# Exp of the scores as the stationary operand of the value products, row sums from a column of ones, and results turned afterwards

## The chip, the cores and the metric

One core of one Trainium2 chip. The metric is device time in microseconds (us) of one execution. A kernel is compared with runs of the kernel before on the same chip.

## The reference, cut to what matters

```python
q, k, v: (8, 12, 448, 64)                    # batch, heads, positions, head size
scores = q @ k^T / 8                         # per batch and head
attn   = exp(scores - max); attn /= attn.sum(-1)
x      = (attn @ v) as (8*448, 12*64)        # 3584 tokens, 768 wide
g, val = x @ w_gate, x @ w_val               # 768 -> 1536 each
out    = (silu(g) * val) @ w_out             # 1536 -> 768
```

Attention is followed by a gated FFN. The kernel works in fp16 with fp32 sums in PSUM (the memory that the matmuls write to), and leaves the maximum out of the softmax.

## The kernel before: the parts that matter

The kernel takes heads two at a time: 48 head pairs, six to a batch. The scores are made transposed, in chunks of 112 keys by 2 x 448 queries, four chunks to a pair; ScalarE takes Exp from PSUM to SBUF. `E` is then the *moving* operand: a group of 16 matmuls in four column tiles makes the products of half the head size of two pairs, and another such group, with a stationary operand of ones, their sums. VectorE inverts the sums and multiplies. What comes out is `X`, features on partitions and tokens beside one another, as the FFN wants it.

```python
ps_s = tile_pool(name="ps_s", bufs=3, space=PSUM)     # score tiles AND gate tiles
ps_f = tile_pool(name="ps_f", bufs=2, space=PSUM)     # products, values, outputs
...
def qk(pr, c):                                        # one score chunk
    s = ps_s.tile([128, 2, 512], FP32, tag="s")
    for hx in range(2):
        nc.tensor.matmul(s[:, hx, 0:S], lhsT=<112 keys>, rhs=<448 queries>, ...)
    nc.scalar.activation(E[pr][:, c], s[0:P, :, 0:S], AF.Exp, scale=sm_scale)

def pv(p0, t):                                        # one group of products
    acc = ps_f.tile([128, 512], FP32, tag="f", name="acc")
    for c in range(NC):
        for j in range(4):
            nc.tensor.matmul(acc[ts(j, 32), 0:S], lhsT=<32 value columns>,
                             rhs=E[p0 + j // 2][:, c, j % 2, :], ...)
...
def ffn1_steps(kk, c0, n, hts):
    for fb in range(NFB):
        gp = ps_s.tile([128, 2, 512], FP32, tag="s", name="gp")[:, 0]   # gate
        for cb in range(NCB): mm(gp[:, 0:n], wslice("g", fb, cb), X[...])
        sg = tanh(gp / 2)                                               # ScalarE
        yield
        vp = ps_f.tile([128, 512], FP32, tag="f")                       # value
        for cb in range(NCB): mm(vp[:, 0:n], wslice("v", fb, cb), X[...])
        ...
```

After a first stage of six pairs, in which attention stands alone, the kernel goes in *visits*: score chunks, then sums or products, then FFN matmuls. A visit issues two or (from pair 8 on) three score chunks, then the sums or products that have become due, then a share of FFN matmuls. TensorE executes in that order.

```python
for x, (chunks, todo) in enumerate(plan):
    for pr, c in chunks:
        qk(pr, c)                     # 3 score tiles: the whole ring ps_s
    ...
    while todo:
        product(*todo.pop(0)[1:])     # sums or products, tiles from ps_f
    ...
    run_fv() / run_o()                # FFN: the first thing is a gate tile, from ps_s
```

The softmax here doesn't subtract the row's maximum and nothing guards it: scores larger than these inputs give would overflow.

## Time and profile before

| | before |
|---|---|
| time, median of 3 runs | 459.06 us (458.02 to 460.3) |
| span of the profiled run | 456.6 us |
| attention groups of 16 tiled matmuls | 72 |
| first gate matmul starts | 29.05 us |
| last of the first 24 Exp ends | 26.70 us |
| waits of gate matmuls for Exp | none in the list of waits |

The lines that show where this kernel is bound are in the prediction. One line more, from the timeline of ScalarE, which sets the pace of the first stage (columns: start, length, instruction, count; in brackets the idle time before it and what ended it):

```profile
6.21 16.83 ACT L212 ACTIVATE E<-s 112x896 f16<-112x896 f32 x20
23.36 3.34 ACT L212 ACTIVATE E<-s 112x896 f16<-112x896 f32 x4 [0.32 <-PE s L205]
```

Twenty Exp without a gap, then 0.32 us idle, then four more, which end at 23.36 + 3.34 = 26.70.

### The profile page before, as it was taken

What the parts mean: (1) busy time and instruction counts of PE and PEld (TensorE: products, weight loads), DVE (VectorE), ACT (ScalarE), POOL (GpSimd) and SP (SyncE); (2) the same over time, 40 slices, a digit from 0 to 9 for tenths busy, and PEclk for the clock granted to TensorE, in tenths of its full rate; (3) what the DMA queues carried; (4) which work ended last, traced back from release to release, by engine and by line L of the source; (5) the groups of instructions that cost most, each with busy time, mean ns of one, the idle gap of its engine ahead of it and who ended that gap; (6) DMA issues with size and microseconds to landing.
All of it is one profiled execution on the core that took longest, in us unless ns stands there. A gap on an engine that the chain in (4) does not pass through costs nothing.

```text
span 456.6 us, 17081 instructions
## 1 busy us (share of the span) xinstructions
PE 448.1 (98%) x7808; PEld 249.5 (55%) x7808; DVE 238.8 (52%) x371; ACT 240.4 (53%) x353; POOL 137.7 (30%) x222
## 2 busy tenths in 40 slices
PE   8899999999999999999999999999999999999996
PEld 3355555444466665555556666455555666544564
DVE  2765764666764645655554546645466356354200
ACT  6986657666653655546354555544565542222222
POOL 8555607853470062601625016510300000000000
PEclk9999999999999999999999999999999999999999
DMA  9999999995955269930947359834222010100133
GB/s 133 195 200 201 178 182 178 217 160 80 128 73 78 48 107 121 143 76 9 128 88 97 59 84 135 127 50 76 33 57 57 23 52 20 54 0 1 36 103 105
DMA packets 82984, 44.43 MB, mean 97 GB/s; under 512 B 37600, under 2 KB 79456, under 8 KB 82912
## 3 DMA queue, kind: packets, MB, share of 16 engines
q0 software_dynamic: 43296, 23.37, 40.2%
q1 hardware_dynamic: 39520, 19.92, 23.9%
q8 instruction: 61, 1.00, 0.9%
q14 instruction: 11, 0.09, 0.1%
q10 hardware_dynamic: 96, 0.05, 0.0%
HBM read 47.19 MB, written 11.01 MB: 127 GB/s over the span
## 4 chain that ended last, share of the span: by engine, by line
PE 85%; DMA 12%; POOL 2%; issue 1%; ACT 0%; POOLq 0%
PE gp L280 18%; PE vp L280 18%; PE op L280 18%; PE acc L225 7%; PE s L205 7%; PE op L277 6%; DMA wv<-in_moe_w_val_dram 5%; DMA wo<-in_moe_w_out_dram 4%; PE gp L277 4%; PE vp L277 4%; PE acc L250 4%; DMA wg<-in_moe_w_gate_dram 2%; POOL q L123 1%; POOL k L123 1%; POOL vt L133 0%
## 5 line engine op out<-in xcount | busy, mean ns | idle before, releaser
L212 ACT ACTIVATE E<-s 112x896 f16<-112x896 f32 x192 | 161.7, 921 | 19.2 <-PE s L205 18.9
L280 PE MATMUL gp<-X,wg 128*32 128x384 f16 (+1 forms) x1848 | 100.7, 351 | 0.0
L280 PE MATMUL vp<-X,wv 128*32 128x384 f16 (+1 forms) x1848 | 100.5, 351 | 0.0
L308 DVE SCALAR_TENSOR_TENSOR t<-sg,gp 128x384 f32<-128x384 f32 (+1 forms) x96 | 59.0, 615 | 74.9 <-ACT sg L296 74.9
L296 ACT ACTIVATE sg<-gp 128x384 f32<-128x384 f32 (+1 forms) x96 | 52.7, 549 | 74.2 <-PE gp L280 48.8
L341 ACT ACTIVATE osb<-op 128x384 f32<-128x384 f32 (+1 forms) x57 | 27.7, 485 | 115.8 <-PE op L280 92.0
L280 PE MATMUL op<-wo,hts 128*32 128x384 f16 x1968 | 87.6, 326 | 0.7 <-issue 0.5
L133 POOL DMA_DIRECT2D vt<-in_v_dram x40 | 26.7, 668 | 158.4 <-PE acc L225 149.7
L265 DVE RECIPROCAL R<-ssb 128x112 f32<-128x112 f32 x92 | 72.8, 826 | 0.6
L280 PEld LDWEIGHTS <-wg 128*32 128x32 f16 x1848 | 52.9, 96 | 35.8 <-issue 0.5
L280 PEld LDWEIGHTS <-wv 128*32 128x32 f16 x1848 | 52.9, 97 | 33.5
L280 PEld LDWEIGHTS <-hts 128*32 128x32 f16 x1968 | 57.0, 97 | 25.7 <-issue 1.1
L311 DVE SCALAR_TENSOR_TENSOR hts<-t,vp 128x384 f16<-128x384 f32 (+1 forms) x96 | 59.6, 621 | 10.4 <-DVE t L308 0.5
L239 DVE TENSOR_TENSOR X<-acc,R 128x448 f16<-128x448 f32 x48 | 29.7, 624 | 45.7 <-PE acc L225 42.1
L205 PE MATMUL s<-qkT 64*128 64x448 f16 x384 | 50.4, 353 | 2.6 <-ACT E L212 1.5
L225 PE MATMUL acc<-E,vt 112*32 112x448 f16 x768 | 45.1, 355 | 0.0
L262 DVE COPY ssb<-acc 128x448 f32<-128x448 f32 x23 | 14.4, 625 | 46.9 <-PE acc L250 46.9
L205 PEld LDWEIGHTS <-qkT 64*128 64x128 f16 x384 | 14.8, 94 | 33.2 <-issue 26.7
L123 POOL DMA_DIRECT2D k<-in_k_dram x42 | 27.9, 663 | 12.6 <-DMA wo<-in_moe_w_out_dram 8.9
L277 PE MATMUL op<-wo,hts 128*128 128x384 f16 (+1 forms) x192 | 29.6, 316 | 0.0
L123 POOL DMA_DIRECT2D q<-in_q_dram x42 | 28.1, 668 | 4.2 <-PE s L205 1.4
L225 PEld LDWEIGHTS <-vt 112*32 112x32 f16 x768 | 17.2, 96 | 21.9 <-issue 12.4
(38 smaller groups left out, 217.4 us busy)
## 6 DMA issues: line engine op xcount, KB each, us to landing
q<-in_q_dram POOLq DMA_DIRECT2D x37, 112.0 KB, 4.7
k<-in_k_dram POOLq DMA_DIRECT2D x37, 112.0 KB, 4.9
vt<-in_v_dram POOLq DMA_DIRECT2D x36, 112.0 KB, 4.2
out_dram<-osb SPq DMA_DIRECT2D x7, 336.0 KB, 3.1
wg<-in_moe_w_gate_dram POOLq DMA_DIRECT2D x8, 288.0 KB, 11.0
wv<-in_moe_w_val_dram POOLq DMA_DIRECT2D x8, 288.0 KB, 11.3
wo<-in_moe_w_out_dram POOLq DMA_DIRECT2D x2, 1152.0 KB, 22.9
out_dram<-osb SPq DMA_DIRECT2D x8, 288.0 KB, 3.8
```

What stands on the lines that cost most here:

```text
L123: nc.gpsimd.dma_start(dst[:, ds(h0, 2 * n)], flat.rearrange("h (p c) d -> p h (c d)", c=NC))
L205: nc.tensor.matmul(s[:, hx, 0:S], lhsT=t[ts(hx, 64)].rearrange("p c q -> p (c q)")[:, c * P : c * P + 128], rhs=t[ts(hx, 64), NC:, :].rear ...
L212: nc.scalar.activation(E[pr][:, c], s[0:P, :, 0:S], AF.Exp, scale=sm_scale)
L225: nc.tensor.matmul(acc[ts(j, 32), 0:S], lhsT=v16[g][:, 2 * r + j % 2, c, :].rearrange("p (d t) -> p t d", t=2)[:, t], rhs=E[p0 + j // 2][: ...
L239: nc.vector.tensor_tensor(X[kk][:, hp + t, ts(bb, S)], acc[:, 0:S], R[p0][:], ALU.mult)
L265: lambda i=i: nc.vector.reciprocal(rt[:, ts(i, P)], ssb[:, ts(i, P)]) for i in range(4)
L277: nc.tensor.matmul(dst, lhsT=lhsT, rhs=rhs, start=start, stop=stop)
L280: nc.tensor.matmul(dst[ts(j, 32), :], lhsT=lhsT[:, ts(j, 32)], rhs=rhs, start=start, stop=stop)
L296: nc.scalar.activation(sg[:, 0:n], gp[:, 0:n], AF.Tanh, scale=0.5)
L308: nc.vector.scalar_tensor_tensor(t1[:, 0:n], sg[:, 0:n], 1.0, gp[:, 0:n], ALU.add, ALU.mult)
L311: nc.vector.scalar_tensor_tensor(hts[:, fb, 0:n], t1[:, 0:n], 0.5 * HS, vp[:, 0:n], ALU.mult, ALU.mult)
L341: nc.scalar.activation(osb[:, ds(m0, w)], op[:, 0:w], AF.Copy, scale=1.0 / HS)
```

## The change

Its intent is to make TensorE's attention work cheaper. `E` becomes the *stationary* operand, 128 query columns at a time, and the values the moving one: 64 columns and a 65th of ones, so that each query's row sum comes out beside its result. That takes the 24 groups of sums away. Per pair there are 32 matmuls of 65 columns. The results come out with queries on partitions, so one reciprocal of 7 columns and a scaling finish them there; then they must be turned: TensorE does it for pairs 0 to 11, a DMA transpose after that. So that each stationary operand has a whole 128 columns, `E` has 15 blocks of 64 queries to a key chunk, seven of each head with a block of zeros between; head 0's queries are taken in rotated order, so that the odd blocks of both heads meet in one product, which needs a second copy of the first 64 queries. The FFN is no longer cut into column tiles, and the reciprocal by Ln and Exp on ScalarE with its table load goes.

```diff
-    def pv(p0, t):
+    def pv(pr):
+        e = Es[pr % NE]
+        vo = Vts[pr % NV]                       # values and a column of ones
         acc = ps_f.tile([128, 512], FP32, tag="f", name="acc")
+        a7 = acc[:, 0 : 7 * (D + 1)].rearrange("p (s d) -> p s d", s=7)
         for c in range(NC):
-            for j in range(4):
-                nc.tensor.matmul(acc[ts(j, 32), 0:S], lhsT=v16[...][:, t], rhs=E[...][:, c, j % 2, :], ...)
+            for j in range(3):
+                for hx in range(2):
+                    nc.tensor.matmul(a7[:, 2 * j + hx], lhsT=<2 blocks of e>, rhs=vo[:, hx, c, 0 : D + 1], ...)
+            for hx in range(2):                 # the odd block, with the zeros
+                nc.tensor.matmul(a7[:, 6], lhsT=<2 blocks of e>, rhs=vo[:, hx, c, 0 : D + 1], ...)
+        nc.vector.reciprocal(r[:, 0:7], a7[:, :, D])
+        nc.vector.tensor_tensor(xt[:, 0:3]..., a7[:, 0:6, 0:D], r[:, 0:6]..., ALU.mult)
+        for hx in range(2):
+            nc.vector.tensor_scalar(xt[0:D, 3, ts(hx, D)], a7[ts(hx, D), 6, 0:D], r[...], None, ALU.mult)
+
+    def turn_x(pr):
+        if pr < XPE:                            # XPE = 12
+            ... 4 matmuls with the identity into ps_f, one VectorE copy into X
+            return
+        nc.sync.dma_start_transpose(...)        # two of them
... (cut: sums(), recips(), scaled(), mm() go; buffers, loads of values, copies into Vts)
         for pr in range(FIRST):                 # first stage
-            if pr in (2, 4): sums of two pairs ... products of two pairs
+            if pr in (2, 4): three copy_v
+            pr 2: pv(0); pr 3: pv(1) turn_x(0), turn_x(1) pv(2)
+            pr 4: turn_x(2) pv(3); pr 5: turn_x(3), pv(4)
...
+            if x == 0:
+                turn_x(4); pv(5); turn_x(5)
-            while todo:
-                product(*todo.pop(0)[1:])
+            for _, p0 in todo:
+                pv(p0) ...
```

What the diff does not show at a glance: 72 groups in the visits and the first stage become 48, one to a pair.

More of the change, by code (lines that the diff above doesn't have):

```diff
@@ L23 @@
 FIRST = 6
-TILED = 8
 WIDE = 8
+XPE = 12
+NE = 4
+NX = 3
+NV = 3
+VS = 6
+EB = 15
 @with_exitstack
@@ L65, in load_table @@
         )
-    load_table("natural_log_exp_and_others")
+    load_table("exp_and_others")
     consts = ctx.enter_context(tc.tile_pool(name="consts", bufs=1))
@@ L71 @@
     attp = ctx.enter_context(tc.tile_pool(name="attp", bufs=4))
-    ep = ctx.enter_context(tc.tile_pool(name="ep", bufs=5))
     xp = ctx.enter_context(tc.tile_pool(name="xp", bufs=2))
@@ L77 @@
     ps_f = ctx.enter_context(tc.tile_pool(name="ps_f", bufs=2, space=PSUM))
-    ones = consts.tile([P, 32], FP16, name="ones")
+    Es = [consts.tile([P, NC * EB + 1, D], FP16, name=f"E{i}") for i in range(NE)]
+    Xts = [consts.tile([128, 4, 128], FP16, name=f"xt{i}") for i in range(NX)]
+    Vts = [consts.tile([P, 2, NC, D + 2], FP16, name=f"vo{i}") for i in range(NV)]
+    vraw = consts.tile([P, VS, 2, NC, D], FP16, name="vraw")
     warm = consts.tile([128, 512], FP16, name="warm")
-    ident = consts.tile([P, P], FP16, name="ident")
+    ident = consts.tile([128, 128], FP16, name="ident")
     wgv = {}
@@ L93 @@
     raw = {}
-    v16 = {}
     qkT = {}
-    E = {}
-    R = {}
     X = {}
@@ L126, in load_qk16, with load_v, copy_v @@
             raw[pr + i] = (q16[:, h : h + 2], k16[:, h : h + 2])
-    def load_v(g, lo=0, hi=2 * GP):
-        b = g // GPB
-        h0 = (g % GPB) * 2 * GP
-        if lo == 0:
-            v16[g] = raws.tile([P, 2 * GP, NC, D], FP16, tag="vt", bufs=3, name="vt")
+    def load_v(pr, n=1):
+        b, h = divmod(2 * pr, H)
         nc.gpsimd.dma_start(
-            v16[g][:, lo:hi],
-            v[b, h0 + lo : h0 + hi].rearrange("h (p c) d -> p h (c d)", c=NC),
-        )
+            vraw[:, ds(pr % VS, n)].rearrange("p r h c d -> p (r h) (c d)"),
+            v[b, h : h + 2 * n].rearrange("h (p c) d -> p h (c d)", c=NC),
+        )
+    def copy_v(pr):
+        nc.vector.tensor_copy(Vts[pr % NV][:, :, :, 0:D], vraw[:, pr % VS])
     def load_w(kind, i):
@@ L143, in load_w @@
             src = (moe_w_gate if kind == "g" else moe_w_val)[:, ts(i, DF // 4)].rearrange(
-                "(a p t) m -> t p a m", p=128, t=2
+                "(t a p) m -> t p a m", p=128, t=2
             )
             for t in range(2):
-                nc.gpsimd.dma_start(wgv[kind, i][:, t::2, :], src[t])
+                nc.gpsimd.dma_start(wgv[kind, i][:, ts(t, NCB // 2), :], src[t])
             return
@@ L161, in prep @@
                     nc.gpsimd.tensor_copy(dst, src)
-        qkT[pr] = attp.tile([128, 2 * NC, P], FP16, tag="qkT", name="qkT", bufs=5)
+        qkT[pr] = attp.tile([128, 2 * S + D], FP16, tag="qkT", name="qkT", bufs=5)
         if pr >= NPE:
             nc.sync.dma_start_transpose(
-                qkT[pr][:], qk16[:].rearrange("p t c h d -> p (t c h d)")
+                qkT[pr][:, 0 : 2 * S].rearrange("p (c q) -> p c q", q=P),
+                qk16[:].rearrange("p t c h d -> p (t c h d)"),
+            )
+            nc.sync.dma_start_transpose(
+                qkT[pr][:, 2 * S :].rearrange("p (c q) -> p c q", c=1),
+                qk16[0:D, 1, 0].rearrange("p h d -> p (h d)"),
             )
@@ L176, in turn0 @@
                             lhsT=qk16[:, 1 - t, c, hx],
-                            rhs=ident[:],
+                            rhs=ident[0:P, 0:P],
                             start=True,
@@ L180, in turn0 @@
                         )
-                dst = qkT[pr][:, ts(1 - t, NC)].rearrange("p (a c) q -> p a (c q)", a=2)
+                dst = qkT[pr][:, ts(1 - t, S)].rearrange("p (a x) -> p a x", a=2)
                 nc.vector.tensor_copy(dst[:, 0], tp[:, 0, 0 : 2 * P])
                 nc.scalar.activation(dst[:, 1], tp[:, 1, 0 : 2 * P], AF.Copy)
+                if t == 0:
+                    nc.vector.tensor_copy(qkT[pr][:, 2 * S :], tp[:, 0, 0:D])
         def turn():
@@ L193, in turn @@
                         src = raw[pr][t][:, hx, c, :]
-                        nc.tensor.transpose(tp[ts(hx, 64), (1 - t) * NC + c, 0:P], src, ident[:])
-            nc.vector.tensor_copy(qkT[pr][:], tp[:, :, 0:P])
+                        nc.tensor.transpose(tp[ts(hx, 64), (1 - t) * NC + c, 0:P], src, ident[0:P, 0:P])
+            nc.vector.tensor_copy(
+                qkT[pr][:, 0 : 2 * S].rearrange("p (c q) -> p c q", q=P), tp[:, :, 0:P]
+            )
+            nc.vector.tensor_copy(qkT[pr][:, 2 * S :], tp[:, NC, 0:D])
         return turn if pr else turn0
     def qk(pr, c):
-        if c == 0:
-            E[pr] = ep.tile([P, NC, 2, S], FP16, tag="E", name="E")
         t = qkT[pr]
@@ L206, in qk @@
                 s[:, hx, 0:S],
-                lhsT=t[ts(hx, 64)].rearrange("p c q -> p (c q)")[:, c * P : c * P + 128],
-                rhs=t[ts(hx, 64), NC:, :].rearrange("p c q -> p (c q)"),
+                lhsT=t[ts(hx, 64), c * P : c * P + 128],
+                rhs=t[ts(hx, 64), ds(S + (1 - hx) * D, S)],
                 start=True,
@@ L211, in qk @@
             )
-        nc.scalar.activation(E[pr][:, c], s[0:P, :, 0:S], AF.Exp, scale=sm_scale)
+        e = Es[pr % NE][:, ds(c * EB, 16)].rearrange("p (h b) x -> p h (b x)", h=2)
+        nc.scalar.activation(e[:, :, 0:S], s[0:P, :, 0:S], AF.Exp, scale=sm_scale)
     def qk_half(pr, half, between=None):
@@ L218, in qk_half @@
                 between()
-    def pv(p0, t):
+    def pv(pr):
+        e = Es[pr % NE]
+        vo = Vts[pr % NV]
         acc = ps_f.tile([128, 512], FP32, tag="f", name="acc")
+        a7 = acc[:, 0 : 7 * (D + 1)].rearrange("p (s d) -> p s d", s=7)
         for c in range(NC):
-            for j in range(4):
-                g, r = divmod(p0 + j // 2, GP)
-                nc.tensor.matmul(
-                    acc[ts(j, 32), 0:S],
-                    lhsT=v16[g][:, 2 * r + j % 2, c, :].rearrange("p (d t) -> p t d", t=2)[:, t],
-                    rhs=E[p0 + j // 2][:, c, j % 2, :],
-                    start=(c == 0),
-                    stop=(c == NC - 1),
-                )
-        return acc
-    def scaled(p0, t, acc):
-        b, hp = divmod(p0, NHP)
+            first, last = c == 0, c == NC - 1
+            for j in range(3):
+                for hx in range(2):
+                    nc.tensor.matmul(
+                        a7[:, 2 * j + hx],
+                        lhsT=e[:, ds(c * EB + 9 * hx + 2 * j, 2)].rearrange("p b x -> p (b x)"),
+                        rhs=vo[:, hx, c, 0 : D + 1],
+                        start=first and j + hx == 0,
+                        stop=False,
+                    )
+            for hx in range(2):
+                b0 = c * EB + 6 + hx
+                nc.tensor.matmul(
+                    a7[:, 6],
+                    lhsT=e[:, ds(b0, 2)].rearrange("p b x -> p (b x)"),
+                    rhs=vo[:, hx, c, 0 : D + 1],
+                    start=False,
+                    stop=last and hx == 1,
+                )
+        r = attp.tile([128, 8], FP32, tag="R", bufs=2, name="R")
+        xt = Xts[pr % NX]
+        nc.vector.reciprocal(r[:, 0:7], a7[:, :, D])
+        nc.vector.tensor_tensor(
+            xt[:, 0:3].rearrange("p j (h d) -> p (j h) d", h=2),
+            a7[:, 0:6, 0:D],
+            r[:, 0:6].unsqueeze(2).to_broadcast([128, 6, D]),
+            ALU.mult,
+        )
+        for hx in range(2):
+            nc.vector.tensor_scalar(
+                xt[0:D, 3, ts(hx, D)], a7[ts(hx, D), 6, 0:D], r[ts(hx, D), 6:7], None, ALU.mult
+            )
+    def turn_x(pr):
+        b, hp = divmod(pr, NHP)
         kk, bb = divmod(b, NB)
@@ L238, in scaled @@
             X[kk] = xp.tile([128, NCB, NB * S], FP16, tag="X", name="X")
-        nc.vector.tensor_tensor(
-            X[kk][:, hp + t, ts(bb, S)], acc[:, 0:S], R[p0][:], ALU.mult
-        )
-    def sums(p0, wide=False):
-        if wide:
-            acc = ps_s.tile([128, 2, 512], FP32, tag="s", name="acc")[:, 0]
-        else:
-            acc = ps_f.tile([128, 512], FP32, tag="f", name="acc")
-        for c in range(NC):
-            for j in range(4):
-                nc.tensor.matmul(
-                    acc[ts(j, 32), 0:S],
-                    lhsT=ones[:],
-                    rhs=E[p0 + j // 2][:, c, j % 2, :],
-                    start=(c == 0),
-                    stop=(c == NC - 1),
-                )
-        R[p0] = attp.tile([128, S], FP32, tag="R", bufs=2, name="R")
-        return acc
@@ L260, in recips @@
-    def recips(p0, acc):
-        ssb = attp.tile([128, S], FP32, tag="ssb", bufs=1)
-        nc.vector.tensor_copy(ssb[:], acc[:, 0:S])
-        rt = R[p0]
-        return [
-            lambda i=i: nc.vector.reciprocal(rt[:, ts(i, P)], ssb[:, ts(i, P)]) for i in range(4)
-        ]
-    def recip_act(p0, acc):
-        ln = attp.tile([128, S], FP32, tag="ssb", bufs=1, name="ln")
-        nc.scalar.activation(ln[:], acc[:, 0:S], AF.Ln)
-        nc.scalar.activation(R[p0][:], ln[:], AF.Exp, scale=-1.0)
@@ L273 @@
-    tiled = [False]
-    def mm(dst, lhsT, rhs, start, stop):
-        if not tiled[0]:
-            nc.tensor.matmul(dst, lhsT=lhsT, rhs=rhs, start=start, stop=stop)
-            return
-        for j in range(4):
-            nc.tensor.matmul(
-                dst[ts(j, 32), :], lhsT=lhsT[:, ts(j, 32)], rhs=rhs, start=start, stop=stop
-            )
+        dst = X[kk][:, hp, ts(bb, S)]
+        xt = Xts[pr % NX]
+        if pr < XPE:
+            tp = ps_f.tile([128, 512], FP32, tag="f", name="xtp")
+            for j in range(4):
+                n = 128 if j < 3 else D
+                nc.tensor.matmul(
+                    tp[:, ds(D + 128 * j if j < 3 else 0, n)], lhsT=xt[:, j], rhs=ident[:, 0:n], start=True, stop=True
+                )
+            nc.vector.tensor_copy(dst, tp[:, 0:S])
+            return
@@ L284, in ffn1_steps @@
+        nc.sync.dma_start_transpose(
+            dst[:, D:S].rearrange("p (j q) -> p j q", j=3), xt[:, 0:3].rearrange("p j m -> p (j m)")
+        )
+        nc.sync.dma_start_transpose(dst[:, 0:D].rearrange("p (j q) -> p j q", j=1), xt[0:D, 3])
     def ffn1_steps(kk, c0, n, hts):
@@ L287, in ffn1_steps @@
             for cb in range(NCB):
-                mm(
+                nc.tensor.matmul(
                     gp[:, 0:n],
@@ L299, in ffn1_steps @@
             for cb in range(NCB):
-                mm(
+                nc.tensor.matmul(
                     vp[:, 0:n],
@@ L333, in ffn2_steps @@
                 for fb in range(NFB):
-                    mm(
+                    nc.tensor.matmul(
                         op[:, 0:w],
@@ L370 @@
         nc.vector.memset(warm[:], 0.0)
-        nc.vector.memset(ones[:], 1.0)
+        for e in Es:
+            nc.vector.memset(e[:, 7::EB], 0.0)
+        for xt in Xts:
+            nc.vector.memset(xt[D:128, 3], 0.0)
+        for vo in Vts:
+            nc.vector.memset(vo[:, :, :, D:], 1.0)
         load_qk16(1, 1)
@@ L376 @@
         load_qk16(4)
-        load_v(0)
-        load_v(1)
+        load_v(0, GP)
+        load_v(3, GP)
         dummy(7)
@@ L396, in emit @@
             elif item[0] == "V":
-                load_v(item[1])
+                load_v(item[1] * GP, GP)
             else:
                 load_w(*item)
-        deferred = []
         ffn2_wait = []
-        def pop_deferred(n=1):
-            for _ in range(n):
-                if deferred:
-                    deferred.pop(0)()
         fvq = []
@@ L425, in run_fv @@
                 next(gen)
-                pop_deferred()
             return 2 * t
@@ L431, in run_o @@
             next(gen)
-            pop_deferred(2)
             return t
@@ L455 @@
                 turn2 = prep(pr + 2)
-            if (pr + 2) % GP == GP - 1 and 4 <= (pr + 2) // GP + 1 < NGRP:
-                load_v((pr + 2) // GP + 1)
             if pr in (2, 4):
-                deferred.extend(recips(pr - 2, sums(pr - 2)))
-                pop_deferred(1)
-            elif pr in (3, 5):
-                halves.append(pv(pr - 3, 1))
-                pop_deferred(4)
-                for t in range(2):
-                    scaled(pr - 3, t, halves[t])
+                for p in range(3):
+                    copy_v(3 * (pr // 2 - 1) + p)
+            elif pr == 3:
+                pv(1)
+                turn_x(0)
+            elif pr == 5:
+                turn_x(3)
             for w in wq.pop(pr, []):
@@ L470 @@
                 dummy(2)
-            if pr in (2, 4):
-                pop_deferred(1)
-                halves = [pv(pr - 2, 0)]
-        p4 = FIRST - 2
-        recip_act(p4, sums(p4, True))
-        load_table("exp_and_others")
-        halves = [pv(p4, t) for t in range(2)]
+            if pr == 2:
+                pv(0)
+            elif pr == 3:
+                turn_x(1)
+                pv(2)
+            elif pr == 4:
+                turn_x(2)
+                pv(3)
+            elif pr == 5:
+                pv(4)
         queue = []
-        for p0 in range(FIRST, NPAIR, 2):
-            for kind, m in (("sums", 8), (0, 11), (1, 14)):
-                queue.append((NC * p0 + m, kind, p0))
+        for p0 in range(FIRST, NPAIR):
+            queue.append((NC * p0 + NC, p0))
         plan = []
@@ L491 @@
                 todo.append(queue.pop(0))
-            todo.sort(key=lambda item: item[1] != "sums")
             plan.append(([divmod(x, NC) for x in range(g, min(g + n, last))], todo))
@@ L496 @@
         for x, (_, todo) in enumerate(plan):
-            for _, kind, p0 in todo:
-                if kind == 1 and p0 % NHP == NHP - 2 and p0 // NHP < B - 1:
-                    adds[x] = p0 // NHP
-        def product(kind, p0):
-            if kind == "sums":
-                pop_deferred(99)
-                deferred.extend(recips(p0, sums(p0)))
-            else:
-                if kind == 0:
-                    pop_deferred(99)
-                scaled(p0, kind, pv(p0, kind))
+            for _, p0 in todo:
+                if p0 % NHP == NHP - 1 and p0 // NHP < B - 1:
+                    adds[x + 2] = p0 // NHP
+        vcopies = {}
+        for x, (_, todo) in enumerate(plan):
+            for _, p0 in todo:
+                vcopies.setdefault(x - 1, []).append(p0)
+        turns = []
         carry = 0.0
@@ L515 @@
             if x == 0:
-                for t in range(2):
-                    scaled(p4, t, halves[t])
+                turn_x(4)
+                pv(5)
+                turn_x(5)
                 add_block(0, end)
-            turn2 = None
+            for p0 in vcopies.get(x, []):
+                copy_v(p0)
             entered = [pr for pr, c in chunks if c == 0]
@@ L525 @@
                     load_qk16(pr + LA, 1)
-                if 4 <= pr // GP + 1 < NGRP:
-                    r = pr % GP
-                    load_v(pr // GP + 1, 2 * r, 2 * r + 2)
+                if 12 <= pr + 3 < NPAIR:
+                    load_v(pr + 3)
             for pr, c in chunks:
@@ L531 @@
                     prep(pr + 2)()
-            any_p = len(todo)
             if x in adds and x > 0:
-                while todo:
-                    product(*todo.pop(0)[1:])
                 add_block(adds[x], end - x)
-            while todo:
-                product(*todo.pop(0)[1:])
+            for _, p0 in todo:
+                pv(p0)
+                if p0 < XPE:
+                    turns.append(p0)
+                else:
+                    turn_x(p0)
             for pr in entered:
@@ L541 @@
                     emit(w)
-            tiled[0] = bool(any_p) and (not chunks or chunks[0][0] >= TILED)
             if adds[max(y for y in adds if y <= x)] < 2:
@@ L559 @@
                     run_o()
-            tiled[0] = False
+            while turns:
+                turn_x(turns.pop(0))
         run_budget(1e9)
-        pop_deferred(99)
+        oq.extend(ffn2_wait)
+        ffn2_wait.clear()
+        for _ in range(3):
+            run_o()
         add_block(B - 1, 1)
```

## The prediction

> **What bounds the kernel now.** I read the page's busy shares first, to see which engine is full.
>
> ```profile
> PE 448.1 (98%) x7808; PEld 249.5 (55%) x7808; DVE 238.8 (52%) x371; ACT 240.4 (53%) x353; POOL 137.7 (30%) x222
> PE   8899999999999999999999999999999999999996
> PEclk9999999999999999999999999999999999999999
> PE 85%; DMA 12%; POOL 2%; issue 1%; ACT 0%; POOLq 0%
> ```
>
> TensorE is full from the second slice on, at full clock, and is 85% of the chain that ended last; VectorE, ScalarE and GpSimd are half idle or more. What is saved on the other engines is worth nothing unless TensorE waits for them. So I turned to the timeline of TensorE alone. Its columns are start, length, instruction. Matmuls overlap and their ends are modelled, so the cost of a group is the start of the next minus its own start, never its length.
>
> ```profile
> 17.50 0.39 PE L194 MATMUL tp<-ident,q 112*64 112x112 f16 x8
> 17.72 0.36 PE L194 MATMUL tp<-ident,k 112*64 112x112 f16 x8
> ...
> 28.56 0.55 PE L205 MATMUL s<-qkT 64*128 64x448 f16 x4
> 29.05 1.15 PE L277 MATMUL gp<-X,wg 128*128 128x384 f16 x6
> 30.03 1.14 PE L277 MATMUL vp<-X,wv 128*128 128x384 f16 x6
> 31.01 1.14 PE L277 MATMUL gp<-X,wg 128*128 128x384 f16 x6
> ...
> 59.73 0.94 PE L250 MATMUL acc<-E,ones 112*32 112x448 f16 x16
> 60.49 1.15 PE L280 MATMUL gp<-X,wg 128*32 128x384 f16 x24
> 61.47 1.15 PE L280 MATMUL vp<-X,wv 128*32 128x384 f16 x24
> 62.55 0.82 PE L205 MATMUL s<-qkT 64*128 64x448 f16 x6
> 63.31 0.94 PE L225 MATMUL acc<-E,vt 112*32 112x448 f16 x16
> 64.46 4.26 PE L280 MATMUL op<-wo,hts 128*32 128x384 f16 x96 [0.21 <-DMA wo<-in_moe_w_out_dram]
> ```
>
> Three readings. One: a group of 16 column-tiled attention matmuls (four quads of 448 columns) takes 60.49 - 59.73 = 0.76 us, 0.77 elsewhere. Two: six full-width FFN matmuls of 384 columns take 0.98 us (30.03 to 31.01), and so do the same six cut into 24 column tiles (60.49 to 61.47): 163 ns per 384 columns, which is 384 at 2.4 per ns and 2.5 ns more. Untiling the FFN gains nothing in itself. Three: 8 transposes with 8 weight loads of 64 columns take 0.22 us, 27 ns a pair of instructions; so TensorE takes in short load-and-multiply pairs at that pace.
>
> Last I read the groups kept apart by shape, for the weight loads (mean ns in the column after the busy time):
>
> ```profile
> L280 PEld LDWEIGHTS <-hts 128*32 128x32 f16 x1968 | 57.0, 97 | 25.7 <-issue 1.1
> L277 PEld LDWEIGHTS <-hts 128*128 128x128 f16 x192 | 18.4, 98 | 11.1
> L194 PEld LDWEIGHTS <-k 112*64 112x64 f16 x80 | 2.6, 110 | 0.0
> ```
>
> A load of 32 columns takes 97 ns, of 64 columns 110, of 128 columns 98. From 32 to 64 columns it grows by 13 ns, so one column costs 0.4 ns on top of a fixed 83 or so; 128 columns should then take 136, but take only what 32 columns do. Full-width loads are read four columns at a time, and occupy the array some 14 ns.
>
> **What the Trainium skill says.** TensorE: Matmul & The Clock Gate, section on weight-path perf modes: fast weight load is on for 128 columns of a type that is not FP32. The 98 ns above agrees, and explains why the change pads each stationary operand to two whole 64-query blocks. The same page, section on the wait between 56 and 53.3 ns: back-to-back matmuls start N / 2.4 GHz + about 2.5 ns apart, never under about 25 ns. The 163 ns above agrees at N = 384; no run here shows N = 65. The same page, back-to-back issue gap, also gives some 81 ns a matmul for load-matmul pairs at N = 128; the 27 ns a pair of the transposes contradicts that as a general floor. TensorEngine Tiling, key properties: changing the tiling mode drains the array. The trace agrees: from the scores, which are row-tiled, the next matmul of another shape comes about 0.1 us later than streaming explains (four row-tiled score matmuls stream in 2 x 0.19 us, yet the FFN follows after 29.05 - 28.56 = 0.49), and about the same is lost on the way in.
>
> **The change part by part.** Before, TensorE holds 24 groups of sums and 48 groups of products: 72 x 0.77 = 55.4 us. All go. With them go 92 RECIPROCAL at 826 ns, 23 copies of sums and 48 scalings on VectorE (72.8 + 14.4 + 29.7 = 117 us), all off the path.
>
> Added on TensorE: per head pair 32 matmuls with 65 moving columns, each with its own 128-column load. Streaming is 65 / 2.4 + 2.5 = 29.6 ns; the 14 ns load goes into the other weight buffer meanwhile. So 32 x 29.6 = 0.95 us a pair, against 55.4 / 48 = 1.155 before: 0.21 us less. All 48 pairs: 45.5 us. The column of ones makes the row sums nearly free (1 column in 65).
>
> Added too: for pairs 0 to 11 the result is turned by TensorE, three matmuls of 128 columns and one of 64: 3 x 56 + 29 = 0.2, say 0.23 us each. Mode switches: I counted the instruction order of both kernels; 154 changes of tiling before, 151 after. Column-tiled stretches vanish, but the row-tiled scores still interrupt: -0.3 us only.
>
> VectorE per pair gets a reciprocal of 7 columns, a 384-column scaling of PSUM (0.56 us, as the 384-column steps of 548 ns), two 64x64 scalings and a 512-column copy of the values: about 1.3 us, 62 us in all, and 12 copies of turned results. It falls from 239 to near 190 us; still idle for half the time. The SP queue gets 72 transposes of results and 37 small ones of the keys; those of the scores took 5.1 us to land, and a result has about 10 us before its FFN block reads it.
>
> Not all of this is on the path. Up to about 26.6 us ScalarE's 24 Exp in a row set the pace, and 9 of the 72 groups lie there, before and after. So count from the first FFN matmul on. Removed: 63 x 0.77 = 48.5. Added: 42 pairs x 0.947 = 39.8, and 6 turns x 0.23 = 1.4. Net -7.3, with switches -7.6.
>
> At that first FFN matmul something is lost. The order is: product of pair 4, scores, turn of 4, product of 5, turn of 5, FFN. Turn 4 waits for VectorE after product 4, turn 5 for VectorE after product 5, and FFN for the copy of turn 5. Nothing is put between. Product 4 ends near 26.4; 1.3 us of latency and VectorE; turn 0.3; product 5 at 28.1 to 29.1; 1.3 us; turn 5; 0.2 latency and 0.6 copy: the FFN starts near 31.5 instead of 29.05, 2.4 us later. (Before, 32 products filled TensorE while the reciprocals were made.)
>
> Sum: 459.1 - 7.6 + 2.4 = 453.9; I say 454.5 for small new waits on value copies early on, where loads still share the DMA engines.
>
> **Rivals.** *The load does not hide.* If load and multiply add up (29.6 + 14 = 44 ns), a pair costs 1.4 us and 42 pairs cost 19 us more: 473, slower. Against it: the 192-column matmuls near the end and the transposes hide their loads. For it: nothing here has a load of full width every 30 ns. Half-hidden, 35 ns, would give 461. *Waits take the gain.* Results now travel over VectorE, SP and a DMA transpose to reach the FFN. If the landing is late at each of the six or so block starts after the turns move to DMA, at 1 to 2 us each, it is 460 to 465. Against it: the block is entered two visits later by design, and DMA is busy under half of the time after 70 us. *DMA sets the early part.* The trace of before shows its first output matmul waiting until 64.41 for the output weights; a faster TensorE would gain nothing before that. Here it is slower up to that point: five products and four turns in place of five groups give +1.8 us, so that matmul should start near 68.7, with no wait. *More gain than counted*: if the 2.4 us were hidden, 451.5; I see no way far below 449.
>
> **Range and chances.** The total hangs on the spacing: each ns is 1.34 us. Spacing 28 to 33 ns with the early wait at 1 to 3 us gives 450 to 459; a tail goes to 35 ns or late transposes. Range 449 to 464. Faster by over 2% means under 449.9: 0.15. Slower means over 468.2, spacing of 40 ns or more: 0.12. Within 2%: 0.73.
>
> **What would show it.** Right: product groups (32 matmuls) spaced 0.95 us from start to start; FFN groups still 0.98 and 1.29; first FFN matmul at 31 to 32 us; first output matmul at 68 to 69 without a DMA wait; VectorE under 45%; TensorE still 97% or more. Wrong: a product group over 1.1 us (load not hidden), TensorE waiting for the transposes of X at block starts, or VectorE ahead of the score copies. If the first FFN matmul starts near 29, the early term is wrong.

## The result

| | before | changed |
|---|---|---|
| median, same chip | 458.6 us (4 runs) | 463.75 us (4 runs, 462.64 to 464.43) |
| span of the profiled run | 456.6 us | 461.3 us |
| TensorE, busy | 448.1 us (98%) | 442.3 us (96%) |
| VectorE, busy | 238.8 us | 207.3 us |
| first gate matmul | 29.05 us | 34.31 us |
| from there to the last matmul's start | 423.7 us | 423.1 us |

The ratio is 1.0105 (95% interval 1.0079 to 1.0131): about 1% slower. Ratios here are the mean time of one kernel's runs over that of the other's in the same rounds, so they are not quite the ratio of the medians quoted. Executions over 1.5% slower than the fastest of the same kernel are left out of the means.

The page of the changed kernel, busy shares and chain first:

```profile
PE 442.3 (96%) x3992; PEld 247.2 (54%) x3992; DVE 207.3 (45%) x480; ACT 237.7 (52%) x350; POOL 137.9 (30%) x222
PE   7879999999999999999999999999999999999996
PEclk9899999999999999999999999999999999999999
PE 93%; ACT 5%; DVE 1%; issue 0%; ACTq 0%
```

TensorE has half as many instructions and is still the bound, but ScalarE now holds 5% of the chain, where it had none, and the first slices have lower digits: 7 8 7 in place of 8 8 9. The second slice lost clock too.

Was the new product slower than thought? A visit in TensorE's timeline, the group first, the FFN after it:

```profile
51.56 0.35 PE L242 MATMUL acc<-vo,E 112*128 112x65 f16 x6
...
52.54 1.14 PE L297 MATMUL gp<-X,wg 128*128 128x384 f16 x6
53.52 1.14 PE L309 MATMUL vp<-X,wv 128*128 128x384 f16 x6
```

From start to start the product takes 52.54 - 51.56 = 0.98 us, 30.6 ns a matmul; six FFN matmuls still take 0.98. No.

So I added up, for each tile written, the time from each matmul's start to the start of the next, from the first gate matmul on:

| us, start to start | before | changed | difference |
|---|---|---|---|
| sums and products | 49.3 | 40.9 | -8.4 |
| turns of results | 0 | 1.8 | +1.8 |
| scores | 38.0 | 46.8 | **+8.8** |
| gate, value, output | 334.8 | 332.1 | -2.8 |
| transposes of q and k | 1.5 | 1.5 | 0 |
| sum | 423.7 | 423.1 | -0.6 |

(Each entry is rounded on its own, so the columns add up only to 0.1.)

The products save what was foretold; the scores give it all back. The scores did not become slower, what follows them did. The list of waits of the changed kernel (us in total, times, longest), TensorE's timeline round one such visit, and ScalarE's line beside it:

```profile
PE gp L297 <- ACT E L225: 8.0, 12, 0.7
```

```profile
138.34 2.11 PE L343 MATMUL op<-wo,hts 128*128 128x384 f16 x12
140.38 0.74 PE L217 MATMUL s<-qkT 64*128 64x448 f16 x6
141.83 1.14 PE L297 MATMUL gp<-X,wg 128*128 128x384 f16 x6 [0.71 <-ACT E L225]
```

```profile
140.87 2.52 ACT L225 ACTIVATE E<-s 112x896 f16<-112x896 f32 x3
```

The visit has no product. Its three score chunks have taken all three tiles of `ps_s`; the gate tile is the fourth request of that ring (a pool whose tiles are handed out in turn), so the gate waits until the first Exp is through: it starts at 140.87, takes some 0.84 to 0.92 us, and the gate starts at 141.83. Of 53 visits of three chunks, 40 hold a product and show no such wait; 13 do not, and the wait stands 12 times. Before, a group with a tile from `ps_f` stood there in almost every visit, 0.77 us of TensorE time that covered that Exp; in the whole trace a gate followed the scores directly only twice, without a wait (0.28 us from the last score's start).

The other part of the loss lies before the first gate matmul: 34.31 - 29.05 = +5.26 us. ScalarE's timeline of the changed kernel:

```profile
6.72 10.02 ACT L225 ACTIVATE E<-s 112x896 f16<-112x896 f32 x12
18.05 1.72 ACT L225 ACTIVATE E<-s 112x896 f16<-112x896 f32 x2 [1.31 <-PE s L217]
20.16 1.73 ACT L225 ACTIVATE E<-s 112x896 f16<-112x896 f32 x2 [0.38 <-PE s L217]
23.17 3.34 ACT L225 ACTIVATE E<-s 112x896 f16<-112x896 f32 x4 [1.29 <-PE s L217]
26.98 3.34 ACT L225 ACTIVATE E<-s 112x896 f16<-112x896 f32 x4 [0.47 <-PE s L217]
```

Exp is no longer unbroken: up to the 24th it waits for scores four times, for 3.45 us in all (before: 0.32), where a product (0.98 us), or a product with a turn and transposes, now stands ahead of the next score chunk. Exp also starts 0.51 us later, at 6.72 in place of 6.21: the second copy of the first 64 queries stands among the copies that the first scores wait for. Together that is why the 24th Exp ends at 30.32 in place of 26.70. After it, TensorE's timeline:

```profile
31.24 0.69 PE L283 MATMUL xtp<-ident,xt 128*128 128x128 f16 x4 [0.41 <-DVE xt L261]
...
33.79 0.69 PE L283 MATMUL xtp<-ident,xt 128*128 128x128 f16 x4 [0.90 <-DVE xt L261]
34.31 1.20 PE L297 MATMUL gp<-X,wg 128*128 128x384 f16 x6
```

The turns of pairs 4 and 5 wait for VectorE, as foretold. Part of the early loss is clock: in the table by stretches (columns: stretch, length, then busy time and count of TensorE, weight loads, VectorE, ScalarE, GpSimd, then granted clock, DMA, GB/s) the two lines of the changed kernel, and after them one of the kernel before:

```profile
11.90:15.30 3.40, 2.05 (x32) 1.20 (x26) 1.22 (x5) 3.40 (x5) 1.53 (x2) 1.00 1.43 195
15.30:18.72 3.42, 3.42 (x46) 2.32 (x45) 1.94 (x7) 2.11 (x3) 1.26 (x2) 0.50 1.41 194
```

```profile
11.90:15.30 3.40, 2.86 (x48) 1.39 (x51) 1.82 (x4) 3.40 (x6) 1.53 (x2) 1.00 1.44 195
```

While Exp sets the pace, TensorE of the changed kernel is busy for 2.05 of 3.40 us (before: 2.86), and for the next 3.42 us it is granted half its clock. The first product, which lies there, takes 1.87 us instead of 0.98.

So: +5.26 early, -0.6 later, together +4.7, the difference of the spans.

### The profile page after: what moved, and what is told of

Same layout as the page of the kernel before. It is cut to its first block, busy times and chain, and to the rows that moved or that the text cites. A ratio compares the mean times of both kernels' runs of the same rounds, so it can differ in the third digit from the quotient of the medians.

```text
span 461.3 us, 9838 instructions
## 1 busy us (share of the span) xinstructions
PE 442.3 (96%) x3992; PEld 247.2 (54%) x3992; DVE 207.3 (45%) x480; ACT 237.7 (52%) x350; POOL 137.9 (30%) x222
## 4 chain that ended last, share of the span: by engine, by line
PE 93%; ACT 5%; DVE 1%; issue 0%; ACTq 0%
PE gp L297 24%; PE op L343 24%; PE vp L309 24%; PE acc L242 9%; PE s L217 8%; ACT E L225 4%; PE acc L251 3%; PE wp L107 1%; PE tp L205 1%; ACT osb L350 1%; PE xtp L283 0%; DVE xt L261 0%; DVE xt L268 0%; DVE qkT L191 0%; DVE R L260 0%
## 5 line engine op out<-in xcount | busy, mean ns | idle before, releaser
L225 ACT ACTIVATE E<-s 112x896 f16<-112x896 f32 x192 | 161.7, 920 | 23.1 <-PE s L217 22.9
L297 PE MATMUL gp<-X,wg 128*128 128x384 f16 (+1 forms) x576 | 124.8, 352 | 8.0 <-ACT E L225 8.0
L309 PE MATMUL vp<-X,wv 128*128 128x384 f16 (+1 forms) x576 | 124.6, 352 | 0.0
L343 PE MATMUL op<-wo,hts 128*128 128x384 f16 (+1 forms) x684 | 115.9, 323 | 0.0
L343 PEld LDWEIGHTS <-hts 128*128 128x128 f16 x684 | 66.3, 98 | 44.1 <-issue 0.4
L309 PEld LDWEIGHTS <-wv 128*128 128x128 f16 x576 | 56.4, 98 | 52.7
L297 PEld LDWEIGHTS <-wg 128*128 128x128 f16 x576 | 53.1, 97 | 55.6 <-issue 12.4
L320 DVE SCALAR_TENSOR_TENSOR hts<-t,vp 128x384 f16<-128x384 f32 (+1 forms) x96 | 59.6, 621 | 10.4 <-DVE t L317 0.5
L242 PEld LDWEIGHTS <-E 112*128 112x128 f16 x1152 | 47.0, 98 | 16.4 <-issue 15.9
L242 PE MATMUL acc<-vo,E 112*128 112x65 f16 x1152 | 52.6, 195 | 0.3 <-DVE X L286 0.3
L251 PE MATMUL acc<-vo,E 112*128 112x65 f16 x384 | 43.2, 194 | 0.0
L134 POOL DMA_DIRECT2D vraw<-in_v_dram x40 | 26.6, 666 | 24.0 <-DVE vo L140 9.9
L261 DVE TENSOR_TENSOR xt<-acc,R 128x384 f16<-128x384 f32 x48 | 26.8, 558 | 1.7
## 6 DMA issues: line engine op xcount, KB each, us to landing
wg<-in_moe_w_gate_dram POOLq DMA_DIRECT2D x8, 288.0 KB, 10.9
```

The costliest lines, as they stand in the source:

```text
L225: nc.scalar.activation(e[:, :, 0:S], s[0:P, :, 0:S], AF.Exp, scale=sm_scale)
L242: nc.tensor.matmul(a7[:, 2 * j + hx], lhsT=e[:, ds(c * EB + 9 * hx + 2 * j, 2)].rearrange("p b x -> p (b x)"), rhs=vo[:, hx, c, 0 : D + 1] ...
L251: nc.tensor.matmul(a7[:, 6], lhsT=e[:, ds(b0, 2)].rearrange("p b x -> p (b x)"), rhs=vo[:, hx, c, 0 : D + 1], start=False, stop=last and h ...
L297: nc.tensor.matmul(gp[:, 0:n], lhsT=wslice("g", fb, cb), rhs=X[kk][:, cb, ds(c0, n)], start=(cb == 0), stop=(cb == NCB - 1),)
L309: nc.tensor.matmul(vp[:, 0:n], lhsT=wslice("v", fb, cb), rhs=X[kk][:, cb, ds(c0, n)], start=(cb == 0), stop=(cb == NCB - 1),)
L320: nc.vector.scalar_tensor_tensor(hts[:, fb, 0:n], t1[:, 0:n], 0.5 * HS, vp[:, 0:n], ALU.mult, ALU.mult)
```

## The experiments

Theory A: the 12 gate waits after score chunks cost the 8 us. Theory B: the first stage costs about 5 us, by clock and by order. The rivals are those of the prediction: weight loads that do not hide (R1), and results that reach `X` late (R2).

Changes against the kernel before, in us, are (ratio - 1) x 458.5 where kernels of different chips are set beside one another.

### 1. Value before gate where a visit has no product (tests A)

```diff
+            v_first[0] = not todo and len(chunks) == 3      # per visit
 ...
-            gp = ps_s.tile(...)  and its matmuls, then vp = ps_f.tile(...)
+            for kind in ("vg" if first == "v" else "gv"):   # first FFN step of that visit only
+                gp from ps_s or vp from ps_f, and its matmuls
```

> One edit on the changed kernel: in the visits of three score chunks that hold no product, the FFN's value matmuls (their PSUM tile is of the small ring) come ahead of the gate matmuls (their tile is of the ring of three that the scores use). Theory A (the gain went into waits of the gate matmuls for a score tile that Exp has not yet freed: 12 waits, 8.0 us of idle, gaps of 0.98 to 1.06 us from scores to gate in place of 0.28): those waits vanish and the time falls by 8 to 9 us, to about 455. Rival B (ScalarE is what runs late there, and the wait only moves to a later place): the waits come back at other lines and the time falls by under 3 us.

Measured: 455.42 us (454.25 to 456.66; before 458.53), ratio 0.9934 (0.9913 to 0.9956). TensorE's timeline at the same place:

```profile
140.22 0.74 PE L218 MATMUL s<-qkT 64*128 64x448 f16 x6
140.89 1.15 PE L305 MATMUL vp<-X,wv 128*128 128x384 f16 x6
141.88 2.11 PE L305 MATMUL gp<-X,wg 128*128 128x384 f16 x12
```

The value matmuls, whose tile is from the other ring, follow the scores without a wait and cover the Exp; the gate starts on time. The gate waits are gone from the list, the scores' sum is 38.7, and from the first gate to the last matmul it takes 415.5 us: 8.2 less than before the change. Against the changed kernel's 423.1 it is 7.6 less, and by the ratios the whole gain is 7.8, a little under the 8 to 9 expected: the same matmuls, with two groups in another order in 13 visits. A holds.

### 2. Dummy matmuls against the half clock (tests B)

```diff
             qk(pr, c)
+            if (pr, c) in ((1, 2), (1, 3), (2, 0), (2, 1), (2, 2)):
+                dummy(1)
```

> One edit on the changed kernel: five extra warm-up matmuls between the score chunks of pairs 1 and 2, so that TensorE is not idle for half of the time from 11 to 15 us. Theory A (the half clock from 15.3 to 18.7 us slows the first product, 1.87 us in place of 0.95, and starves Exp for 1.3 us): the clock stays at 1.0, and the time falls by 1 to 1.5 us, to about 462.5. Rival B (the first stage waits for the values, which land at 14.8 us, whatever the clock): no change.

Measured: 461.65 us (461.61 to 464.5), ratio 1.0085 (1.0055 to 1.0115). In the profiled run the clock is full throughout, TensorE is busy for all of the 3.40 us from 11.90, the first gate starts at 32.84 (1.5 earlier), and the span is 459.8, also 1.5 less. The ratio's interval overlaps that of the changed kernel, so by time alone the gain is not resolved. The mean clocks of the single runs go with their times: one of the four, the one of 464.5, has 0.996, the other three 0.999 to 1.000 and 461.61 to 461.69 us. A mean of 0.996 fits one stretch of half clock (3.4 / 2 of 461 us), and all four runs of the changed kernel have it. The extra matmuls are not shown to be what keeps the clock, though: in experiments 6 and 9, whose first stage is that of the changed kernel and no busier (2.04 of 3.40 us), the profiled run had full clock up to the first gate, which started at 32.88, and in experiment 6 all four runs have a mean of 1.000. In a profile with it, the half clock cost the first stage some 1.4 us; what brings it on stays open.

### 3. The products and turns of the first stage spread out (tests B)

```diff
-            qk_half(pr, 0, prep(2) if pr == 1 else None)
+            early = {4: 1, 5: 2}
+            qk_half(pr, 0, prep(2) if pr == 1 else (lambda: turn_x(early[pr])) if pr in early else None)
 ...  pv(2) moved from pair 3 to pair 4, turn_x(0) between half pairs
             if x == 0:
-                turn_x(4)
                 pv(5)
+                turn_x(4)
                 turn_x(5)
```

> One edit on the changed kernel: in the first stage products and turns no longer follow each other at once; each stands between other score chunks, and product 5 comes ahead of turn 4. Theory A (blocks of 1.3 to 1.7 us without a score matmul starve Exp there, which has three score tiles to live from; and turns wait for VectorE): the first gate matmul moves from 34.3 to about 31.5 us, and the time falls by 2 to 3 us, to about 461. Rival B (the first stage is bound by the sum of TensorE's work in it, so that moving it about gives nothing): first gate matmul still near 34, no change.

Measured: 460.73 us (460.64 to 461.88), ratio 1.0056 (1.0041 to 1.0071): 2.2 us better than the changed kernel by the ratios. In the profiled run, the slowest of the four, the first gate started at 33.05, not at the 31.5 expected. Two things are in that. First, TensorE ran slowly for longer at the start of this run: eight transposes at 7.74 take 0.37 us from start to start, where experiment 2 has 0.22 at 7.21, and Exp then waits 1.12 us up to 9.76. The trace's record of the granted clock begins only at 10.15 us here, in experiment 2 at 4.52, in the kernel before and the changed one near 5; before its first entry a table of stretches shows full clock because nothing is recorded, not because it was granted. The profiles of experiments 1, 4 and 5 begin as late (9.70 to 10.18) and have the same gap; no other profile has one of over 0.4 us there. Without these 1.1 us the first gate would come near 31.9 (an estimate). Second, gaps of 0.21, 0.45, 1.10 and 0.45 us between Exp remain; the 1.10 has the product of pair 3 behind a value copy that queues on VectorE. So the order does cost, but the edit recovered only a part of it, and how large a part one profile does not settle.

### 4. All three edits together

> The three edits together. If they are independent as theory A has it, their gains add up: 8.5 + 1.2 + 2.5 = 12 us, so about 451.5, faster than the kernel before (458.6) by 1.5%. If the early stage is bound by loads of weights instead (rival), the sum falls short by the 3 to 4 us of the two early edits: about 455.

Measured: 453.47 us (453.22 to 454.33), ratio 0.9890 (0.9873 to 0.9906). By the ratios the three edits alone give 7.8 + 0.9 + 2.2 = 10.9 us over the changed kernel, together 9.9: they nearly add up, so A and B are separate losses. Two us of the 451.5 expected are missing, all in the first stage (first gate at 33.12); some 1.1 of them, in the profiled run, are the late start of the clock named under experiment 3.

### 5. A narrower stationary operand (tests R1)

For the middle two key chunks the stationary operand is cut to 96 columns. Its output is wrong, which doesn't matter for the time.

```diff
+            m = 128 if first or last else 96
-                        a7[:, 2 * j + hx], lhsT=e[...]
+                        a7[0:m, 2 * j + hx], lhsT=e[...][:, 0:m]
```

> The changed kernel with the stationary operand of the middle two of the four key chunks cut from 128 columns to 96 (the result is wrong on purpose in the last 32 rows of each block). Theory (as the prediction read it off the load durations: full-width loads take four columns at a time, others one every 0.4 ns): 96 columns take 40 ns and no longer hide behind the 29.6 ns of 65 moving columns, so those 16 matmuls of each pair start 40 ns apart while the other 16 stay at 29.6, and the 48 pairs cost 768 x 10.4 ns = 8 us more. Rival: the load hides anyway[...], and a narrower operand changes nothing.

Measured: 481.23 us in the profiled run, which was slow (mean clock 0.979), and 473.44 in the other, at full clock. That one is 9.2 us over what the changed kernel's ratio gives on this chip (459.38 x 1.0105 = 464.2, an estimate; there is no run of the changed kernel beside it). The half clock in the trace ends at 43.8 us; a product far behind that, in TensorE's timeline, and the groups of weight loads by shape (after the busy time, the mean ns of one):

```profile
160.47 0.43 PE L243 MATMUL acc<-vo,E 112*96 112x65 f16 x6
...
160.83 0.35 PE L243 MATMUL acc<-vo,E 112*128 112x65 f16 x6
...
161.07 1.14 PE L298 MATMUL gp<-X,wg 128*128 128x384 f16 x6
```

```profile
L243 PEld LDWEIGHTS <-E 112*96 112x96 f16 x576 | 35.4, 130 | 0.0
L243 PEld LDWEIGHTS <-E 112*128 112x128 f16 x576 | 25.5, 102 | 16.0 <-issue 15.5 <-DVE t L318 0.4
```

A chunk is eight matmuls (the two of the odd blocks are cut from the lines). With 96 columns it takes 160.83 - 160.47 = 0.36 us, 45 ns a matmul; with 128 columns 161.07 - 160.83 = 0.24, 30 ns. Fewer columns, same streaming, half as long again (40 ns were expected): with 96 columns the load is not hidden, with 128 it is. R1 is out for the changed kernel by its own 30.6 ns, and the padding to 128 columns is worth 15 ns x 32 = 0.48 us a pair; 768 such matmuls make 11.5 us, near the 9.2 of the time. (The means of the groups hold the early half-clock stretch too, for both shapes; from 44 us on they are 125 and 98 ns.)

### 6. All results turned by TensorE (tests R2)

```diff
-XPE = 12
+XPE = 48
```

> One edit on the changed kernel: all 48 results are turned by TensorE, none by DMA. Theory: a turn costs TensorE 0.2 to 0.25 us and nothing else waits for it, so 36 more cost 7 to 9 us, to about 472. Rival (the DMA transposes delay something, so that taking them away gives back): clearly under 7 us more.

Measured: 468.85 us (468.77 to 469.07), ratio 1.0213 (1.0195 to 1.0232), 5.0 us more than the changed kernel. It still has 12 gate waits, of 7.6 us. By the time alone that would be the rival's sign, clearly under 7. The trace tells them apart: from the first gate on it takes 7.0 us more, as expected, and 1.4 comes back in the first stage, which had no half clock in this run. The turns' sum rises by 10.4 and that of the output matmuls falls by 2.4, as the switch to the row-tiled scores now follows a turn: 8.0 us for 36 turns, 0.22 us each. Taking the DMA transposes away removes no wait, so R2 is out: their landing cost the changed kernel nothing.

### 7. The edits together, with the first stage mended further

Beside the three edits: six value tiles instead of three, the value copies of pairs 3 to 5 a pair earlier, the second copy of the first 64 queries ahead of ScalarE's half, and the transposes of pair 8 between the last two turns.

```diff
-NV = 3
+NV = 6
 ...
             if x == 0:
                 pv(5)
                 turn_x(4)
+                prep(8)()
                 turn_x(5)
```

> The three edits together, and four more in the first stage: six value buffers in place of three (the product of pair 3 waited 0.59 us for a value copy that waited for the product of pair 2), the copy of the first 64 queries ahead of ScalarE's half (first Exp 0.5 us late), and the transposes of pair 8 between turn 4 and turn 5. If the rest of the early loss is in these waits, the first gate matmul comes 1.5 to 2.5 us earlier than 33.1, and the time is 451 to 452, against 453.5 for the three edits. If the early stage is simply full on TensorE, 453 to 453.5.

Measured: 453.17 us (452.93 to 453.27, 4 runs; before 459.38), ratio 0.9870 (0.9853 to 0.9888). The span is 451.5, the 24th Exp ends at 28.77 and the first gate starts at 31.96. It is the fastest of all, 1.3% ahead of the kernel before. Against experiment 4 the interval overlaps, so a gain over that is not shown by the time. The first gate comes 1.2 us earlier than in experiment 4's profile, but that one had lost 1.1 to the late clock. The 451 to 452 hoped for was missed; 453.17 lies where it was expected if the first stage is simply full on TensorE.

### 8. The same with DMA transposes from pair 6 on

```diff
-XPE = 12
+XPE = 6
```

> As the one before, and the results of pairs 6 to 11 turned by DMA too, while weights still load. If the first FFN block that needs them (near 88 us) finds them landed, 6 x 0.23 = 1.4 us less; if the transposes queue behind the weights, TensorE waits at that block for the landing and the time is the same or worse.

Measured: 460.37 us (459.0 to 461.25), ratio 1.0029 (1.0008 to 1.0050), 7 us worse than version 7. Its list of waits:

```profile
PE gp L307 <- DMA X<-xt: 4.7, 1, 4.7
```

One wait of 4.7 us, at 88 us: five gate matmuls of a new block had run, and the sixth waited for the last slice of `X`, a DMA transpose, to land. The half clock followed it, from 92.6 to 96.0, and the next six value matmuls took 2.60 us, twice their usual 1.3. So R2's mechanism exists. Between 50 and 100 us these transposes took 2.8 us at the least, 6.8 in the median and 11.7 at most from issue to landing. Turning pairs 6 to 11 by TensorE at 0.22 us each is what keeps it out of the changed kernel.

### 9. Every product after the FFN of its visit (A, the other way)

If A is right, the wait must come in nearly every visit of three chunks once the products no longer stand between the scores and the gate.

```diff
-            for _, p0 in todo: pv(p0) ...        # ahead of the FFN
             ... run_fv() / run_o()
+            for _, p0 in todo: pv(p0) ...        # behind it
```

> One edit on the changed kernel, to make the suspected wait more frequent: in every visit the products stand after the FFN work of the visit instead of between the scores and the gate matmuls. Then 52 visits of three score chunks, in place of 12, go straight from scores to gate. Theory A: each of the 40 new ones costs 0.70 to 0.78 us, as the 12 did, so 28 to 31 us more: about 493. Rival B (ScalarE's own lateness, not the place of the product, makes the wait): the number of waits stays near 12 to 20, and under 6 us more. Results reach their FFN block one visit later, which may add a few us of waits for transposes at the seven block starts; these would show under their own name.

Measured: 495.62 us (494.81 to 496.42, 2 runs; before 458.09), ratio 1.0816 (1.0769 to 1.0862). Its list of waits:

```profile
PE gp L297 <- ACT E L225: 31.1, 48, 0.7
```

48 waits where there were 12, at 0.65 us in the mean (0.67 there). They account for 31.1 - 8.0 = 23.1 us. The products' sum rises from 40.9 to 50.2, 9.3 more: the switch to the row-tiled scores falls behind most of them now (1.06 us in place of 0.98), and the turns of pairs 6 to 11, directly behind their products, wait for VectorE (9 waits of turns, 7.1 us, in place of 3, 1.7 us). Together that is 32.4 of the 34.8 us by which the time from the first gate on grew. (The span grew by 33.3, as the first stage had full clock and was 1.4 shorter.) A half clock from 32.85 to 36.26 us is in the rest: the first gate and value groups took 1.90 and 1.71 us in place of 0.98.

## Why the prediction was wrong

It foretold 454.5 us, a gain of 1%; the kernel lost 1%. The range held the result, the direction did not. Its sum was -7.6 + 2.4 = -5.2 us, and +4.7 was measured in the spans: of the 9.9 between them 7.0 lie from the first gate on, and 2.9 before it.

**The product's cost was right.** Foretold 0.95 us a pair, measured 0.98; 42 pairs for 39.8 us, measured 40.9. Turns at 0.23 us: 0.29 from start to start (1.75 for six), 0.22 net in experiment 6. The groups removed for 48.5 us: 49.3. The net from the first FFN matmul on, -7.6, is there once the waits are gone: experiment 1 has -8.2. That the two are so close is in part luck. There products and turns give -6.6 (foretold -7.3); the scores rise by 0.7 and the FFN falls by 2.3, where -0.3 was foretold for all switches; where the 2.3 comes from was not looked into. FFN groups stayed at 0.98. One reading that the cost leaned on was weaker than it looked: the transposes at "27 ns a pair" are in two tiles of 64 columns (shape 112*64), and their starts come in twos, 3 ns apart, every 49 ns. They did not show that a full-width load hides every 30 ns; the product's own 30.6 did.

**The step that failed: the sum took -7.6 us as a change on the path without asking what the removed groups had covered.** It has terms for the groups removed and added and for the switches, and none for what comes to stand next to one another where a group is gone. A group between three score chunks and a gate was not only 0.77 us of work; it was the time in which ScalarE freed the gate's tile. Of the 72 groups 24 went without a successor, and in 12 visits the gate then stood directly behind the scores. What showed it: 8.0 us of waits named in the trace, gone by exchanging two groups (experiment 1), grown to 31.1 by moving the rest (9). The rival "waits take the gain" was right in its name and in its size (460 to 465), but wrong in its place: it looked at the landing of `X`, where the changed kernel has no wait at all.

**The early term was mis-sized: 2.4 us foretold, 5.3 measured.** The waits of turns 4 and 5 for VectorE were foreseen. Not foreseen was that "ScalarE's 24 Exp in a row set the pace" until 26.6 us would stop being true. In the profiles without half clock before the gate (6 and 9) the first gate starts at 32.88, 3.8 late: 2.2 because the 24th Exp ends at 28.89, not 26.70 (0.5 of them the later first Exp, the rest the stalls), and 1.6 because the tail from there to the gate is 3.99 us in place of 2.35. So the foretold part, the tail, was even a little smaller than 2.4; the late and stalled Exp was not counted. The half clock, 1.4 us more in the profiled run, was not thought of. First output matmul: foretold 68 to 69, measured 71.76, without a DMA wait as foretold.

**VectorE's fall was mis-sized, without effect.** Foretold near 190 us, measured 207.3: the four steps of a pair take 26.8 + 26.7 + 15.0 + 9.9 = 78.4 us in all, 1.63 us a pair and not 1.3. The two scalings of 64 x 64 at 278 ns each were the dearest surprise. It is idle for over half of the time; its length counts only at turns 4 and 5.

**The rivals.** "The load does not hide" is refuted at 128 columns, and experiment 5 shows how near it was: 96 columns cost 15 ns more a matmul. "DMA sets the early part" has nothing for it. TensorE's 96% instead of the foretold 97% or more was the sign of the waits.

What stays open: how much of the first stage's loss is the order of products and turns alone, as the state of the clock differs between profiles of it; and why the half clock comes in some runs with the same TensorE load and not in others, and the first full clock later in some.

## What to carry to other kernels

Before you take work out of the engine that sets the pace, ask what waits that work was covering: look at what stands before and behind it, and whether the one behind needs a buffer that the one before has just filled. In a ring of three buffers shared by two uses, a burst of three by one makes the other wait for a whole consumer step; put work that draws on another ring between them, which may cost only an exchange of two groups. And count a stage by the engine that paces it: bunching TensorE work ahead of a score chunk there costs ScalarE's time, though TensorE itself has room.

## What the Trainium skill lacked or had wrong

- TensorE: Matmul & The Clock Gate, back-to-back issue gap: some 81 ns per matmul for pairs of load and multiply at N = 128 does not hold as a floor. In the turns, pairs with 128 moving columns and a full load each start 56 ns apart in the trace (three in a row), and 32 pairs with 65 moving columns ran at 30.6 ns each (0.98 us).
- The same page, weight-path perf modes: right that 128 columns is what matters, but it does not say what missing it costs between matmuls. Here, at full clock, loads of 32, 64, 96 and 128 columns took 97, 110, 125 and 98 ns, and the products' matmuls stood 45 ns apart with 96 columns, 30 with 128.
- The same page, on the clock gate: the window of some 3.4 us agrees (half clock from 15.30 to 18.72). Its rule of no idle gaps over about 3.4 us is not enough: the window before was busy for 2.05 of 3.40 us and half clock followed, though not in every run. Its second failure mode, frequent short idling, is the nearer description; it gives no busy share, and two runs with 2.04 us busy in the same stretch kept the full clock (where their windows began, the trace does not say).
- VectorE: DVE Perf Modes, the table of cycles: 120 + columns at 0.96 GHz from PSUM makes an estimate of 192 ns for 64 columns; the 64 x 64 scalings took 278. For 384 columns the estimate is 525, measured 558. It has no row for reciprocals: 206 ns for 7 columns (826 for 112 before).
- TensorEngine Tiling, key properties: the drain on a mode switch has no figure. In experiment 9 a product took 1.06 us up to row-tiled scores behind it, and in the changed kernel 0.98 up to a gate: 0.08 us for the switch.
- No page has the wait, two uses of one PSUM ring: 0.67 us each time in the changed kernel. Perfetto Trace Analysis comes nearest, with a line on repeating gaps as a sign of too few buffers.
